# Attention scores on four array tiles at once, with groups of heads scheduled in twos: a block-summary attention followed by two feed-forward layers

## The chip, the cores and the metric

One core of one Trainium2 chip runs the whole kernel in one launch. The metric is device time in microseconds (us), from the runs of the compiled kernel; the profile shows one execution of it, whose span goes from the first to the last instruction. TensorE (PE) multiplies matrices into PSUM; VectorE (DVE), ScalarE (ACT) and GpSimd (POOL) do everything else; SyncE (SP) issues most of the DMAs. Each engine works through its own list of instructions in order.

## What is computed

An attention over a local window of 32 keys and over 24 block summaries, then two layers without bias. Shapes: q, k, v 2 x 8 x 768 x 64 (batch, head, token, dimension), w_in 512 x 2048, w_out 2048 x 512 for each layer; all fp32.

```python
k_sum = k.reshape(B, H, nb, 32, D).max(axis=3)
v_sum = v.reshape(B, H, nb, 32, D).mean(axis=3)
scores_l = where(abs(i - j) < 16, scale * q @ k.T, -1e9)
scores_s = scale * einsum('bhsd,bhnd->bhsn', q, k_sum) + log(32)
a = softmax(concat(scores_l, scores_s))
x = (a @ concat(v, v_sum)).transpose(0, 2, 1, 3).reshape(1536, 512)
h = x @ w_in;  x = maximum(0.01 * h, h) @ w_out          # layer 1
h = x @ moe2_w_in;  out = (h * tanh(softplus(h))) @ moe2_w_out   # layer 2
```

## The kernel before, in words

**Attention** is cut into 24 groups of 256 tokens of a pair of heads (`groups`: batch, chunk of 256 tokens, head pair). A group passes through these steps, each a function:

- `k_window` (POOL, L257): a tile `kw` of four windows, each 96 keys and the 24 block maxima of k from `k_sum` (DVE, L298).
- `scores` (PE, L362): 8 fp32 matmuls, for each of 4 blocks of 64 queries and each head of the pair. Head 0 lies in SBUF partitions 0 to 63, head 1 in 64 to 127, and their outputs go to the same partitions of PSUM, so the two heads use the two 64x64 tiles on the diagonal of the array. The result, 128 x 480, takes one PSUM bank.
- `score_max` (DVE, L374): adds the mask, scales, finds the row maximum, once for each of the 4 blocks; then the bank is free. `score_exp` (ACT, L384) with sums, `score_inv` (DVE, L393, L394), `score_norm` (POOL, L399).
- `p_transpose` (PE, L405) into another bank, `p_evac` (ACT L413 or DVE L415) to `pT`, `av` (PE, L424: 8 matmuls with a window of v and the v sums, into the same bank), `x_part` twice (a cast to fp32r, ACT L441 or DVE L443, and the remainder by subtraction, DVE L439). Then that bank is free.

The v sums come from `sum_v0` (PE, L317) for batch 0, spread to the four tiles `vw` by `place_v0` (DVE L327, ACT L329), and from `sum_vs` (DVE, L340) for batch 1.

**The layers** keep fp32 precision by high and low parts. A weight block is loaded as raw 64-bit words (`raw`), its top taken by ACT (`w_scale`, L130), merged on DVE (`w_merge`, L137), then split into a high part (`w_hi`, ACT L166 or DVE L164) and a low one (`w_lo`, POOL L173). `up` (PE, L458) makes one 128-wide block of h for 256 or 512 tokens in 12 matmuls, in two halves; `leaky_a` (ACT, L469, L470) and `leaky_b` (DVE, L474) make g; `down` (PE, L513) adds it into the four banks y0 to y3. One `up` is a slot; its `down` follows 3 slots later (`LAG`). Slots 0 to 5 have 256 tokens and need groups 0 to 3 (slots 0 to 2) and 4 to 7 (slots 3 to 5); slots 6 to 8 need groups 0 to 7, slots 9 to 14 groups 8 to 15, slots 15 to 20 groups 16 to 23.

**What sets the order.** Attention and slots 0 to 14 are not written in program order. `step(...)` notes every piece with an engine and a cost in us, what it needs, a `turn` (when it is due, counted in slots) and what it takes from `store` and gives back: PSUM banks, tiles `kw`, `s`, `pT`, raw buffers. `run_order` replays the steps in a time of its own, gives each free engine the ready step with the lowest turn, and so writes the list of each engine. The turn of a group's scores is `first_score[g]`, from the table `RATE`; its transposes and the product with v are due 0.3 slots later. Where TensorE would be idle before the first `up`, `warm` puts matmuls on a zero tile (L220). Banks: a0, a1 and y0 to y3 serve attention until slot 2 has been issued; from then on y0 to y3 belong to `down`, and a0 and a1 alone serve scores and transposes. From slot 15 on a plain loop writes the rest.

```python
            S1[g] = step({"PE": (1.15, 0)}, f, [KX[g], Q[g]], u, [("bank", ("S", g))], [("kw", g)])
            MX[g] = step({"dve": (0.88, 0)}, later(score_max, g), [S1[g]], u, [("s", ("s", g))], [("S", g)])
```

Of the kernel before, what the change touches and what calls it, by code (L numbers as in the profile page):

```python
# [28 lines left out]
def kernel(  # L29
# [34 lines left out]
    RATE = (2, 1, 1, 1, 1, 1, 2, 2, 1, 2, 1, 2, 1, 1)  # L64
# [142 lines left out]
    mask = ap1.tile([P, 6, WN], F32, name="mask")  # L207
# [53 lines left out]
    def k_window(g, part):  # L261
# [5 lines left out]
        w = ap2.tile([P, NB, WN], F32, tag="kw", bufs=3, name="kw")  # L267
# [98 lines left out]

    def score_max(g):
        b, c, hp = groups[g]
        pS = st[g]
        m0 = 0 if c == 0 else (2 if c == S // GT - 1 else 1)  # L370
# [2 lines left out]
        for n in range(NB):
# [44 lines left out]
    def av(g):  # L418
# [3 lines left out]
        for n in range(NB):  # L422
            for s in range(2):
# [144 lines left out]
    if True:  # L568
# [30 lines left out]
        first_score = {0: -4, 1: -4, 2: -4, 3: -4, 4: -1}  # L599
        g = 5  # L600
        for i, c in enumerate(RATE):
            for _ in range(c):
                first_score[g] = i
                g += 1
        assert g == NG
        X = len(RATE) + 1

# [7 lines left out]
        def step(on, fn, needs=(), turn=0.0, take=(), give=(), tag=None):  # L615
# [66 lines left out]
        for g in range(NG):  # L682
            b, c, hp = groups[g]
            u = first_score[g] + (g / 10 if g < 4 else 0)
            if g > 3:
                Q[g] = load(later(load_q, g, SP), 0.131, [S1[g - 4]], u - 2.5)
            KW[g] = step({"pool": (0.71, 1)}, later(k_window, g, 0), [K[b, hp]], u - 0.9, [("kw", ("kw", g))])
            KX[g] = step({"pool": (0.28, 1)}, later(k_window, g, 1), [KW[g], KS[b, hp]], u - 0.9)
            if g > 3:
                KW[g].needs.append((NM[g - 4], 0.07))  # L690

            def f(eng, g=g):
                scores(g, held["S", g])
            S1[g] = step({"PE": (1.15, 0)}, f, [KX[g], Q[g]], u, [("bank", ("S", g))], [("kw", g)])
            MX[g] = step({"dve": (0.88, 0)}, later(score_max, g), [S1[g]], u, [("s", ("s", g))], [("S", g)])
            EX[g] = step({"act": (1.6, 0)}, later(score_exp, g), [(MX[g], -0.5)], u)
            IV[g] = step({"dve": (0.39, 0)}, later(score_inv, g), [EX[g], MX[g]], u)
            NM[g] = step({"pool": (1.0, 1)}, later(score_norm, g), [IV[g]], u)

            def f(eng, g=g):  # L700
                p_transpose(g, held["T", g])
            TR[g] = step({"PE": (0.45, 0)}, f, [NM[g]], u + 0.3, [("bank", ("T", g))], [("s", g)])

            def f(eng, g=g):
                p_evac(g, eng)
            PT[g] = step({"act": (0.59, 0), "dve": (0.69, 0)}, f, [TR[g]], u + 0.3, [("pT", ("pT", g))])
            if g > 3:
                n = [AV[g - 4]]
                VW[g] = load(later(load_vw, g, SP), 0.196, n, u - 1.5)
                if (b, c) == (1, 0):  # L710
                    PLACE[b, hp] = step({"act": (0.83, 0)}, later(place_vs, hp), n + [VSS[4 * (hp // 2) + 3]], u - 0.5)
            AV[g] = step({"PE": (0.5, 0)}, later(av, g), [PT[g], VW[g], PLACE[b, hp]], u + 0.3, (), [("pT", g)])
            w = list(KX.values())[:12] if g >= 16 else []

            def f(eng, g=g):
                x_part(g, 0, eng)
            XH[g] = step({"act": (0.38, 0), "dve": (0.42, 0)}, f, [AV[g]] + w, u + 0.3)
            XL[g] = step({"dve": (0.43, 0)}, later(x_part, g, 1, None), [XH[g]], u + 0.3, (), [("T", g)])
# [294 lines left out]
```

## Time and profile before

| | |
|---|---|
| runs | 614.77, 614.79, 615.48 us; median 614.79 |
| span of the profiled execution | 612.8 us, 9138 instructions |
| its own time beside the span | not listed apart; the median of the runs is 2.0 us above the span |
| busy | PE 605.0, weight loads 492.2, DVE 386.0, ACT 314.6, POOL 196.1 us |
| DMA | 52.10 MB, mean 85 GB/s |
| granted TensorE clock | 1.00 |

A row of the timeline gives the start, the duration, engine, line, operation, result and inputs, partitions and elements, and how many such instructions were merged; in brackets stands what the engine waited for before it. TensorE lists fp32 matmuls as two instructions each, so 8 matmuls of a group are x16. Matmuls overlap: the time to the start of the next row is what a row costs, its own duration is longer by the end of the last matmul.

### The profile page before, as it was taken

The numbers are of one execution on the slowest core, as the hardware profiler recorded it, in microseconds if no ns is written. First come the engines' busy times: TensorE is split into PE (matmuls) and PEld (weight loads), VectorE is DVE, ScalarE is ACT, GpSimd is POOL, SyncE is SP. The second block draws the span as 40 slices with busy tenths as digits, with TensorE's granted clock in tenths as the row PEclk, the third lists the DMA queues.
The fourth block names the chain that finished last, engine by engine and source line by source line (L and its number), as shares of the span: only waits on it lengthen the run. The fifth ranks groups of instructions, "written<-read, shape, count | busy, mean of one in ns | idle before, by whom it ended". The sixth has DMA issues, their size and how long they took to land.

```text
span 612.8 us, 9138 instructions
## 1 busy us (share of the span) xinstructions
PE 605.0 (99%) x3330; PEld 492.2 (80%) x3330; DVE 386.0 (63%) x779; ACT 314.6 (51%) x669; POOL 196.1 (32%) x214
## 2 busy tenths in 40 slices
PE   9899999999999999999999999999999999999997
PEld 7788888778788888888888888888888888888886
DVE  6799775466242114112726798877689998678685
ACT  4786876457554123213656655454457555434442
POOL 6575673074330001001532133233231322332221
PEclk9999999999999999999999999999999999999999
DMA  9996463027541000001346410000012000001011
GB/s 320 344 287 224 135 207 113 2 94 247 164 156 60 1 1 1 0 1 34 110 137 235 130 43 1 0 1 0 1 40 99 0 1 1 1 18 52 1 70 68
DMA packets 19373, 52.10 MB, mean 85 GB/s; under 512 B 2176, under 2 KB 5248, under 8 KB 19072
## 3 DMA queue, kind: packets, MB, share of 16 engines
q1 hardware_dynamic: 18752, 51.00, 25.5%
q8 instruction: 26, 0.43, 0.3%
q10 hardware_dynamic: 576, 0.52, 0.3%
q14 instruction: 19, 0.16, 0.1%
HBM read 48.37 MB, written 3.15 MB: 84 GB/s over the span
## 4 chain that ended last, share of the span: by engine, by line
PE 89%; DMA 5%; DVE 3%; ACT 2%; issue 0%; POOL 0%; SPq 0%; DVEq 0%; ACTq 0%
PE h L458 41%; PE y L520 21%; PE y L513 20%; PE a L362 3%; DMA raw<-in_moe_w_in_dram 2%; PE a L424 2%; DMA v<-in_v_dram 2%; PE a L405 2%; DVE mid L137 1%; PE y L534 1%; ACT top L130 1%; DMA kT<-in_kT_dram 1%; DVE pT L415 0%; DVE ks L298 0%; DVE x L439 0%
## 5 line engine op out<-in xcount | busy, mean ns | idle before, releaser
L458 PE MATMUL h<-x,w 128*128 128x512 f32 (+1 forms) x1188 | 288.0, 388 | 0.0
L458 PEld LDWEIGHTS h<-x,w 128*128 128x128 f32 x1188 | 217.8, 188 | 48.9
L513 PE MATMUL y<-g,w 128*128 128x512 f32 (+1 forms) x612 | 145.9, 384 | 0.8 <-ACT yp L550 0.8
L520 PE MATMUL y<-w,g 128*128 128x512 f32 x552 | 136.9, 394 | 0.0
L194 POOL TENSOR_TENSOR g<-e,g 128x512 fp32r<-128x512 f32 x47 | 73.6, 1566 | 187.1 <-ACT g L191 175.8
L513 PEld LDWEIGHTS y<-g,w 128*128 128x128 f32 x612 | 109.8, 188 | 25.7 <-ACT yp L550 1.3
L520 PEld LDWEIGHTS y<-w,g 128*128 128x128 f32 x552 | 103.7, 188 | 24.1
L173 POOL TENSOR_TENSOR w<-mid,w 128x512 fp32r<-128x512 f32 x45 | 63.3, 1413 | 117.6 <-ACT w L166 113.8
L474 DVE TENSOR_TENSOR g<-t,g 128x512 fp32r<-128x512 f32 (+1 forms) x51 | 36.8, 721 | 90.9 <-ACT g L470 90.9
L137 DVE SCALAR_TENSOR_TENSOR mid<-raw,top 128x512 int32<-128x512 int32 x64 | 55.3, 869 | 33.1 <-POOL w L173 24.5
L469 ACT ACTIVATE t<-h 128x512 f32<-128x512 f32 (+1 forms) x51 | 28.9, 567 | 88.7 <-PE h L458 88.2
L130 ACT ACTIVATE top<-raw 128x512 f16<-128x512 bf16 x64 | 50.9, 795 | 38.1 <-DMA raw<-in_moe_w_out_dram 15.3
L485 ACT ACTIVATE e<-h 128x512 f32<-128x512 f32 x48 | 28.7, 598 | 68.9 <-PE h L458 62.3
L496 DVE SCALAR_TENSOR_TENSOR u<-u,r 128x512 f32<-128x512 f32 x48 | 36.9, 769 | 25.5 <-ACT r L489 25.2
L488 ACT ACTIVATE r<-u,two 128x512 f32<-128x512 f32 x48 | 34.8, 724 | 30.5 <-DVE u L487 30.5
L384 ACT ACTIVATE s<-s,nm 128x120 f32<-128x120 f32 x96 | 36.7, 385 | 16.0 <-DVE nm L374 12.1
L166 ACT CAST w<-mid 128x512 fp32r<-128x512 f32 x61 | 37.0, 614 | 8.6 <-DVE mid L137 4.2
L191 ACT CAST g<-e 128x512 fp32r<-128x512 f32 x48 | 29.5, 615 | 19.4 <-DVE e L498 19.1
L399 POOL TENSOR_TENSOR s<-s,r 128x480 f32<-128x480 f32 x24 | 25.1, 1047 | 33.1 <-DVE r L394 27.7
L487 DVE SCALAR_TENSOR_TENSOR u<-e 128x512 f32<-128x512 f32 x48 | 34.6, 720 | 1.1
L497 DVE SCALAR_TENSOR_TENSOR u<-u,r 128x512 f32<-128x512 f32 x48 | 33.1, 691 | 1.4
L498 DVE SCALAR_TENSOR_TENSOR e<-e,u 128x512 f32<-128x512 f32 x48 | 33.1, 689 | 1.1
(70 smaller groups left out, 467.2 us busy)
## 6 DMA issues: line engine op xcount, KB each, us to landing
raw<-in_moe_w_in_dram SPq DMA_DIRECT2D x32, 512.0 KB, 3.9
raw<-in_moe_w_out_dram SPq DMA_DIRECT2D x32, 512.0 KB, 3.8
vw<-in_vW_dram SPq DMA_DIRECT2D x24, 192.0 KB, 5.2
kT<-in_kT_dram SPq DMA_DIRECT2D x8, 400.0 KB, 7.0
out_dram<-yp SPq DMA_DIRECT2D x12, 256.0 KB, 2.0
q<-in_qT_dram SPq DMA_DIRECT2D x20, 128.0 KB, 4.0
vS<-in_vS_dram SPq DMA_DIRECT2D x2, 1024.0 KB, 7.1
v<-in_v_dram SPq DMA_DIRECT2D x2, 768.0 KB, 9.4
```

The lines of the kernel that those rows point to most:

```text
L130: nc.scalar.mul(out=do, in_=di, mul=4.0)
L137: nc.vector.scalar_tensor_tensor(out=d, in0=wraw.pop(i)[:, 0:2 * DM].rearrange("p (f w) -> p f w", w=2)[:, :, 1], scalar=13, in1=wtop.pop( ...
L166: nc.scalar.copy(out=w[:, 0], in_=wmid[i])
L173: (eng or nc.gpsimd).tensor_sub(out=w[:, 1], in0=wmid.pop(i), in1=w[:, 0].bitcast(F32))
L194: (nc.vector if lo == "dve" else nc.gpsimd).tensor_sub(out=dst_lo, in0=src, in1=dst_hi.bitcast(F32))
L384: nc.scalar.activation(out=s[:, n], in_=s[:, n], func=AF.Exp, scale=-1.0, bias=nm[:, n:n + 1], accum_out=sm[:, n:n + 1],)
L458: nc.tensor.matmul(ph[:, 0:n], w[:, a, kt * P:(kt + 1) * P], x[:, c, kt, o:o + n], start=(kt == 0 and i == 0), stop=(kt == KT - 1 and i == 2),
L474: nc.vector.tensor_sub(out=g[:, 1, 0:n], in0=t[:, 0:n], in1=g[:, 0, 0:n].bitcast(F32))
L488: nc.scalar.activation(out=r, in_=u, func=AF.Ln, bias=two[:, 0:1])
L496: V.scalar_tensor_tensor(out=u, in0=u, scalar=2.0, in1=r, op0=ALU.add, op1=ALU.mult)
L513: mm = nc.tensor.matmul(y[d][:, o:o + n], w[:, a, d * P:(d + 1) * P], g[:, c, 0:n], start=sta and not second, stop=sto,)
L520: nc.tensor.matmul(y[d], g[:, a, d * P:(d + 1) * P], w[:, c], start=sta, stop=sto,)
```

## The change

`scores` takes one group or two. For each pair of blocks and each head it issues two matmuls with the same SBUF partitions, whose outputs go to the lower and the upper half of the PSUM partitions: all four 64x64 tiles of the array are used. Tiles of different heads write to different banks, so there is a bank for each head (`pS[0]`, `pS[1]`), and a group fills half of both. The first four groups are scored one by one, the other twenty in ten pairs. In a pair, `score_max`, `score_exp` and the transposes stay steps of one group, while `scores` and `av` are one step for both; both banks are given back when the second mask pass is done. Order of rows within `s` changes from block to head and block, so the mask has 3 variants in place of 6 and `av` picks other columns. The table `RATE` now lists the turns of the ten pairs; `kw` has 4 buffers for 3, the dummy tile is 128 columns wide, and `run_order` can hand out two banks to one step. In the changed file lines after `scores` stand 7 lower: L362 is L367, L405 L412, L424 L431, L458 L465, L513 L520.

```diff
-    RATE = (2, 1, 1, 1, 1, 1, 2, 2, 1, 2, 1, 2, 1, 1)
+    RATE = (-1.0, -0.5, 3.5, 4.0, 6.5, 7.0, 7.0, 9.5, 10.5, 13.0)
...
-    mask = ap1.tile([P, 6, WN], F32, name="mask")
+    mask = ap1.tile([P, 3, WN], F32, name="mask")
...
-    def warm(n, w=256):
+    def warm(n, w=128):
...
-        w = ap2.tile([P, NB, WN], F32, tag="kw", bufs=3, name="kw")
+        w = ap2.tile([P, NB, WN], F32, tag="kw", bufs=4, name="kw")
...
-    def scores(g, tag):
-
-        t = qin.pop(g)
-        w = kwin.pop(g)
-        pS = bank(tag)
-        for n in range(NB):
-            for s in range(2):
-                r = slice(s * D, (s + 1) * D)
-                nc.tensor.matmul(
-                    pS[r, n * WN:(n + 1) * WN], t[r, :, n], w[r, n, :], start=True, stop=True,
-                )
-        st[g] = pS
+    def scores(gs, tags):
+
+
+        pS = [bank(t) for t in tags]
+        for k, g in enumerate(gs):
+            t = qin.pop(g)
+            w = kwin.pop(g)
+            for m in range(NB // 2):
+                o = (k * (NB // 2) + m) * WN
+                for s in range(2):
+                    r = slice(s * D, (s + 1) * D)
+                    for e in range(2):
+                        n = 2 * m + e
+                        nc.tensor.matmul(
+                            pS[s][e * QB:(e + 1) * QB, o:o + WN], t[r, :, n], w[r, n, :], start=True, stop=True,
+                        )
+            st[g] = (pS, k)
...
+            h, m = divmod(i, NB // 2)
+            o = (k * (NB // 2) + m) * WN
+            v = 1 if c == 0 and m == 0 else (2 if c == S // GT - 1 and m == NB // 2 - 1 else 0)
             nc.vector.tensor_tensor_reduce(
-                out=s[:, n], in0=pS[:, n * WN:(n + 1) * WN], in1=mask[:, m0 + n],
-                scale=-1.0 / rscale, scalar=BIG, op0=ALU.add, op1=ALU.min, accum_out=nm[:, n:n + 1],
+                out=s[:, i], in0=pS[h][:, o:o + WN], in1=mask[:, v],
+                scale=-1.0 / rscale, scalar=BIG, op0=ALU.add, op1=ALU.min, accum_out=nm[:, i:i + 1],
             )
...
+        batches = [[g] for g in range(4)] + [[g, g + 1] for g in range(4, NG, 2)]
+        first_score = {g: u for gs, u in zip(batches, (-4, -4, -4, -4) + RATE) for g in gs}
+        X = 15
...
+            t = [("bank", ("S", gs[0], h)) for h in range(2)] + [("s", ("s", g)) for g in gs]
+            x = step(
+                {"PE": (1.3 if pair else 0.8, 0)}, f, [d[g] for g in gs for d in (KX, Q)], u, t, [("kw", g) for g in gs],
+            )
...
+                MX[g] = step(
+                    {"dve": (0.88, 0)}, later(score_max, g), [x] + ([MX[gs[0]]] if g > gs[0] else []), u, (),
+                    [("S", gs[0], h) for h in range(2)] if last else (),
+                )
...
+            y = step({"PE": (1.1 if pair else 0.6, 0)}, f, n, u + 0.3, (), [("pT", g) for g in gs])
```

Since `run_order` writes the lists, the change moves instructions on every engine. Three places follow, each before and then as changed; a name ends in the number of its allocation.

VectorE before the first layer matmul, around the first merge of weights (L137). Before:

```order
L327 COPY vw_99<-y_283 24x512
L443 CAST x_373<-y_263 128x256
L393 TENSOR_SCALAR r<-sm 128x4
L394 RECIPROCAL r<-r 128x4
L439 TENSOR_TENSOR x_373<-y_263,x_373 128x256
L443 CAST x_373<-a_343 128x256
L137 SCALAR_TENSOR_TENSOR mid<-raw,top_86 128x512
L439 TENSOR_TENSOR x_373<-a_343,x_373 128x256
```

As changed:

```order
L400 TENSOR_SCALAR r<-sm 128x4
L401 RECIPROCAL r<-r 128x4
L137 SCALAR_TENSOR_TENSOR mid<-raw,top_86 128x512
L400 TENSOR_SCALAR r<-sm 128x4
L401 RECIPROCAL r<-r 128x4
L327 COPY vw_99<-y_309 24x512
L422 COPY pT<-y_366 120x512
L450 CAST x_401<-a_269 128x256
```

The merge stood behind the copies to vw and two casts to x; now it stands ahead of them, between two reciprocals.

TensorE around the first layer-1 matmul (`h<-x`), with the scores of groups 4 and 5 (kw with q_102 and q_103). Before:

```order
L405 MATMUL a_422<-ident,s 120x128 x4
L362 MATMUL a_429<-kw,q_102 64x120 x8
L424 MATMUL a_422<-pT,vw_101 64x64 x8
L458 MATMUL h<-x_373,w 128x256 x6
L362 MATMUL a_474<-kw,q_103 64x120 x8
L362 MATMUL a_489<-kw,q_104 64x120 x8
```

As changed:

```order
L431 MATMUL y_366<-pT,vw_100 64x64 x8
L412 MATMUL a_420<-ident,s 120x128 x4
L465 MATMUL h<-x_401,w 128x256 x6
L431 MATMUL a_420<-pT,vw_101 64x64 x8
L367 MATMUL a_461<-kw,q_102 64x120 x2
L367 MATMUL a_462<-kw,q_102 64x120 x2
L367 MATMUL a_461<-kw,q_102 64x120 x2
L367 MATMUL a_462<-kw,q_102 64x120 x2
L367 MATMUL a_461<-kw,q_103 64x120 x2
```

The layer matmuls now stand ahead of the last single group's product with v, and the scores of groups 4 and 5, which stood on both sides of them, follow as one block that alternates between two banks.

TensorE from slot 6 to slot 7 (ups of 512 tokens). Before:

```order
L458 MATMUL h<-x_373,w 128x256 x12
L362 MATMUL a_972<-kw,q_102 64x120 x8
L458 MATMUL h<-x_373,w 128x512 x6
L405 MATMUL a_1009<-ident,s 120x128 x4
L513 MATMUL y_725<-g,w 128x256 x3
L513 MATMUL y_726<-g,w 128x256 x3
L424 MATMUL a_1009<-pT,vw_100 64x64 x8
```

As changed:

```order
L431 MATMUL a_947<-pT,vw_98 64x64 x8
L431 MATMUL a_955<-pT,vw_99 64x64 x8
L465 MATMUL h<-x_401,w 128x512 x12
L412 MATMUL a_1036<-ident,s 120x128 x4
L412 MATMUL a_1042<-ident,s 120x128 x4
L520 MATMUL y_728<-g,w 128x256 x3
L520 MATMUL y_729<-g,w 128x256 x3
L431 MATMUL a_1036<-pT,vw_100 64x64 x8
L431 MATMUL a_1042<-pT,vw_101 64x64 x8
```

Single groups stood between halves of ups and downs; now two transposes and two products with v stand together, and no scores are among these rows.

## Rows read from the trace of the kernel before

**Rows 1.** The page, busy time and share of the span of each engine, with instructions.

```profile
PE 605.0 (99%) x3330; PEld 492.2 (80%) x3330; DVE 386.0 (63%) x779; ACT 314.6 (51%) x669; POOL 196.1 (32%) x214
```

**Rows 2.** Stages: length, busy PE, PEld, DVE, ACT, POOL, then clock, DMA share, GB/s.

```profile
24.73:39.88 15.15, 14.67 (x191) 13.13 (x187) 12.54 (x54) 12.96 (x48) 11.34 (x18) 1.00 1.04 305
39.88:64.31 24.43, 24.36 (x248) 21.78 (x247) 23.94 (x78) 18.36 (x62) 13.72 (x24) 1.00 0.68 212
64.31:76.53 12.22, 12.22 (x151) 10.23 (x149) 8.91 (x43) 10.67 (x36) 8.80 (x14) 1.00 0.52 158
76.53:126.59 50.06, 50.06 (x429) 39.89 (x425) 25.90 (x111) 29.05 (x94) 18.25 (x28) 1.00 0.31 99
126.59:612.80 486.21, 481.75 (x2080) 389.62 (x2076) 298.25 (x436) 230.65 (x388) 129.59 (x86) 1.00 0.17 56
```

**Rows 3.** Timeline of TensorE: start us, us, engine, line, operation, tiles, count.

```profile
13.53 0.85 PE L317 MATMUL y<-v,ind 128*24 128x128 f32 x24
...
25.73 2.18 PE L362 MATMUL a<-kw,q 64*64 64x120 f32 x32
27.84 0.97 PE L458 MATMUL h<-x,w 128*128 128x256 f32 x6
...
38.73 1.22 PE L362 MATMUL a<-kw,q 64*64 64x120 f32 x16
39.88 0.97 PE L513 MATMUL y<-g,w 128*128 128x256 f32 x6
...
47.51 0.69 PE L424 MATMUL a<-pT,vw 120*64 120x64 f32 x16
48.13 0.99 PE L458 MATMUL h<-x,w 128*128 128x256 f32 x6
...
56.96 0.60 PE L405 MATMUL a<-ident,s 128*120 128x128 f32 x4
57.32 0.96 PE L513 MATMUL y<-g,w 128*128 128x256 f32 x6
```

**Rows 4.** The same timeline, cut at 13.70, 39.05 and 39.10 us.

```profile
13.53 0.42 PE L317 MATMUL y<-v,ind 128*24 128x128 f32 x8
...
38.73 0.50 PE L362 MATMUL a<-kw,q 64*64 64x120 f32 x4
...
38.73 0.62 PE L362 MATMUL a<-kw,q 64*64 64x120 f32 x6
```

**Rows 5.** Timeline of all engines up to the first layer-1 matmul.

```profile
15.86 0.85 PE L317 MATMUL y<-v,ind 128*24 128x128 f32 x24 [0.33 <-DMA v<-in_v_dram]
16.79 1.40 DVE L327 COPY vw<-y 24x512 f32<-24x512 f32 x2 [0.31 <-PE y L317]
...
18.28 1.17 ACT L329 COPY vw<-y 24x512 f32<-24x512 f32 x2 [0.75 <-PE y L424]
...
21.25 0.68 DVE L137 SCALAR_TENSOR_TENSOR mid<-raw,top 128x512 int32<-128x512 int32 x1
...
24.73 0.98 PE L458 MATMUL h<-x,w 128*128 128x256 f32 x6
```

**Rows 6.** Groups by shape, 0 to 131 us: count, busy us, mean ns, idle before.

```profile
L384 ACT ACTIVATE s<-s,nm 128x120 f32<-128x120 f32 x96 | 36.7, 385 | 16.0 <-DVE nm L374 12.1 <-POOL kw L257 3.6
L399 POOL TENSOR_TENSOR s<-s,r 128x480 f32<-128x480 f32 x24 | 25.1, 1047 | 33.1 <-DVE r L394 27.7 <-ACT pT L413 2.3 <-ACT vw L346 1.7
...
L439 DVE TENSOR_TENSOR x<-a,x 128x256 fp32r<-128x256 f32 x23 | 9.6, 423 | 4.7 <-ACT x L441 4.1
L340 DVE TENSOR_REDUCE vs<-vS 128x16 f32<-128x512 f32 x8 | 8.4, 1054 | 0.0
...
L415 DVE COPY pT<-a 120x512 f32<-120x512 f32 x11 | 7.6, 689 | 4.1 <-PE a L405 4.0
```

**Rows 7.** Timeline of VectorE: a mask pass of one group and what follows.

```profile
44.57 0.28 DVE L374 CUSTOM_DVE_ANT_0 s<-a,mask 128x120 f32<-128x120 f32 x1
...
45.38 1.81 DVE L298 TENSOR_REDUCE ks<-kT 128x24 f32<-128x768 f32 x2
```

More of the change, by code (lines that the diff above doesn't have):

```diff
@@ L205 @@
     kp = att.enter_context(tc.tile_pool(name="kp", bufs=4))
-    mask = ap1.tile([P, 6, WN], F32, name="mask")
+    mask = ap1.tile([P, 3, WN], F32, name="mask")
     vw = [ap1.tile([WN, NB, 2, D], F32, name=f"vw{i}") for i in range(H // 2)]
     idle = {}
-    def warm(n, w=256):
+    def warm(n, w=128):
         if not idle:
-            idle["t"] = ap1.tile([P, 256], F32, name="idle")
+            idle["t"] = ap1.tile([P, 128], F32, name="idle")
             nc.vector.memset(idle["t"], 0.0)
@@ L235, in build_const @@
         nc.gpsimd.memset(mask[:, 0, WK:WN], math.log(SB) * rscale)
-        nc.vector.tensor_copy(out=mask[:, 1:], in_=mask[:, 0:1].to_broadcast([P, 5, WN]))
-        nc.gpsimd.memset(mask[:, 0, 0:HALO], NEG * rscale)
-        nc.gpsimd.memset(mask[:, 5, WK - HALO:WK], NEG * rscale)
+        nc.vector.tensor_copy(out=mask[:, 1:], in_=mask[:, 0:1].to_broadcast([P, 2, WN]))
+        nc.gpsimd.memset(mask[0:QB, 1, 0:HALO], NEG * rscale)
+        nc.gpsimd.memset(mask[QB:P, 2, WK - HALO:WK], NEG * rscale)
         nc.gpsimd.memset(two, 2.0)
@@ L352 @@
     st = {}
[L354 to L365 removed]
+    def scores(gs, tags):
[13 more added lines that the diff above has]
+            st[g] = (pS, k)
     def score_max(g):
         b, c, hp = groups[g]
[L369 to L370 removed]
+        pS, k = st[g]
         s = ap2.tile([P, NB, WN], F32, tag="s", bufs=4, name="s")
         nm = ap2.tile([P, NB], F32, tag="nm", bufs=4, name="nm")
[L373 removed]
+        for i in range(NB):
+            h, m = divmod(i, NB // 2)
+            o = (k * (NB // 2) + m) * WN
+            v = 1 if c == 0 and m == 0 else (2 if c == S // GT - 1 and m == NB // 2 - 1 else 0)
             nc.vector.tensor_tensor_reduce(
[L375 to L376 removed]
+                out=s[:, i], in0=pS[h][:, o:o + WN], in1=mask[:, v],
+                scale=-1.0 / rscale, scalar=BIG, op0=ALU.add, op1=ALU.min, accum_out=nm[:, i:i + 1],
             )
@@ L426, in av @@
                     w[:, n, s, :],
-                    t[:, n, s * QB:(s + 1) * QB],
+                    t[:, s * (NB // 2) + n // 2, (n % 2) * QB:(n % 2 + 1) * QB],
                     start=True, stop=True,
@@ L575 @@
             load_k(0, hp, SP)
-        warm(5)
+        warm(10)
         build_const()
@@ L598 @@
         NI = len(items)
[L599 to L606, printed above, removed]
+        batches = [[g] for g in range(4)] + [[g, g + 1] for g in range(4, NG, 2)]
+        first_score = {g: u for gs, u in zip(batches, (-4, -4, -4, -4) + RATE) for g in gs}
+        X = 15
         steps = []
@@ L681 @@
         S1, KX, MX, EX, IV, NM, TR, PT, AV, XH, XL = ({} for _ in range(11))
[L682 to L718, printed above, removed]
@@ L720 @@
         for g in range(1, NG):
             for d in (KW, S1):
-                d[g].needs.append((d[g - 1], -9.0))
+                if d[g] is not d[g - 1]:
+                    d[g].needs.append((d[g - 1], -9.0))
         for i in range(2 * nA + 4):
@@ L847, in run_order @@
                     for name, key in x.take:
-                        have = store[name]
+                        have = list(store[name])
                         if name == "bank":
                             have = [y for y in have if y[0] == "a" or not closed[0]]
+                        for other, item in pick.values():
+                            if other == name:
+                                have.remove(item)
                         if not have:
```

44 lines of the change are left out of this document (43 added, 1 removed).

## The prediction

> **What bounds the kernel now.** First the table of busy times on the page: TensorE 605.0 of 612.8 us, the next engine, VectorE, 386.0 [rows 1]. Then the stages, over five stretches [rows 2]. TensorE is hardly idle after 24.73 us: 14.67 busy of 15.15, 24.36 of 24.43, then all of 12.22 and 50.06. So from the first layer-1 matmul (24.73 us, L458) on, time that TensorE no longer needs comes off the end, unless a wait takes its place. Before 24.73 us TensorE is filled with dummy matmuls (L220), and a chain through the other engines decides. The same table shows what lies closest behind: VectorE, busy 23.94 of 24.43 us between 39.88 and 64.31. The profiled span is 612.8 us, the median of the runs 614.79; the 2.0 us around the span I leave as they are, and take the sum off the median. The granted clock reads 1.00 in every stretch, so I charge no change of it.
>
> **The scores themselves.** One group takes 1.15 us from its first matmul to the next instruction's (38.73 to 39.88) and 16 passes: each of its 8 fp32 matmuls runs as two [rows 3]. Two passes (one on each diagonal 64x64 tile) are in flight at a time: the same row cut at two ends shows 4 passes in 0.50 us and 6 in 0.62 [rows 4], so a round is 0.12 us, and 8 rounds plus 0.19 us for changing over make the 1.15. The change puts four passes in a round. No row has four 64x64 tiles. Lower bound: the sums of v (L317) keep four column tiles in flight, 8 passes in 0.42 us and 24 in 0.85, which is 0.43 / 4 = 0.107 us a round [rows 3, 4], for passes of 128 columns instead of 120. Upper bound: no overlap, two groups in a row as now, 25.73 to 27.84, 2.11 us. I take the four-tile row, as the nearest, but the longer round of L362: a pair is 32 passes, 8 rounds of 0.12 plus 0.2, **1.2 us**; a single group 0.7.
>
> A rule speaks against it. The trace has column tiles that share all their rows with loads and matmuls overlapping: L424 does 16 passes between 47.51 and 48.13, 39 ns a pass, and L317 27 ns [rows 3, 4]. The Trainium skill (TensorE: Matmul & The Clock Gate, Part 3, what overlaps and what doesn't) says that a weight load overlaps running matmuls only where the row group differs; in the new order two neighbours always share their row group. By that rule a pair would stay near 2.1 us; by L317 and L424, where no row group differs, it does not hold here.
>
> **The sum, stage A, up to the first L458 matmul.** Now: the merge of the first weights (L137) is issued on VectorE only at 21.25, behind the casts to x; its cast and its low part follow, and TensorE begins at 24.73 [rows 5]. In the new order of VectorE that merge stands before the copies to vw (the first pair of fences above), so the weights are ready some 5 us sooner. What is late next is v: its second load releases L317 at 15.86, hidden by nothing, as before. From there: sums 0.85, first copy to vw on ScalarE 0.58, second on VectorE 0.70, two more on ScalarE 1.17 [rows 5], cast to x (taken as long as the subtraction) and subtraction 0.42 each [rows 6], a handover of some 0.05 before each: 15.86 + 4.14 + 0.2 = 20.2. Stage A: **-4.5 us**. Bounds: 0 (some queue still holds it) to -4.7 (no handover).
>
> **Stage B, from there to the first matmul of slot 8 (now 76.53).** The order lists between these two marks give the counts. The layer matmuls are the same (ups 0 to 7, downs 0 to 5). Scores: now 12 groups, then 6 pairs: 12 x 1.15 - 6 x 1.2 = 6.6 us less. Transposes: 11 then 8, at 0.36 (56.96 to 57.32) [rows 3] to 0.45 with a change of mode: 1.3 less. Products with v (L424): 11 groups at 0.62 = 6.8, then one group and 4 pairs; a pair is 16 rounds less one changeover, 1.1: 5.0, so 1.8 less. Sum 9.7 less TensorE work; it now takes 51.8 us with 0.55 idle (15.15 - 14.67 and 24.43 - 24.36), so 41.5 are left.
>
> New waits must be added, because pairs come in lumps. I follow the first two pairs with durations of rows: exponentials 4 x 0.385 a group on ScalarE, the scaling 1.05 on GpSimd, the copy of the transposed tile 0.69, a sum of v 1.05 [rows 6], the mask pass of a group 0.8 (44.57 to 45.38) [rows 7]. (1) The first pair takes both banks a0 and a1, and a1 still holds the last single group until its x is written: v product, 0.6, cast and subtraction 0.85, so TensorE waits 1.0. (2) The low weights of slot 1: 0.3. (3) The transpose of group 5: its exponentials end some 3.6 us after the pair's mask begins, its reciprocal is queued on VectorE behind the mask pass of group 6, then the scaling; TensorE has 0.4 of transposes left: 1.0. (4) The paired v product waits for both copies, and that of group 4 sits on VectorE behind the mask pass of group 7 and a sum of v: 1.3. (5) Low weights of down 0: 0.4, and 0.5 of small change. Together 4.5 us. From slot 3 on the ups and downs between two steps of a pair (1.5 us and more each) are longer than what the pair waits for. Stage B: 41.5 + 4.5 - 51.8 = **-5.8 us**. Bounds: no waits (-10.3) and twice the waits (-1.3).
>
> **Stage C, slot 8 to the end of attention (now 126.59).** Work moved here from B comes back: 3 transposes (+1.3), 6 pairs of v products for 9 groups (+1.0); 4 pairs of scores for 7 groups, 4.8 for 8.05 (-3.3). **-1.0 us**, no waits: VectorE has 25.90 of 50.06 us busy [rows 2]. After it the same instructions run; TensorE works 481.75 of 486.21 us there, and what it waits for starts from the end of attention, so it moves along.
>
> Edits at nothing: the smaller mask (its copy shrinks to two fifths, on VectorE before k has landed); the fourth kw buffer; dummy matmuls of 128 columns, twice as many; q loads, which SP issues by groups as before and whose release comes sooner.
>
> Sum: -4.5 - 5.8 - 1.0 = -11.3. **614.8 - 11.3 = 603.5 us.** With the upper price of a pair instead (2.11) 10 x 0.9 = 9 us of it are lost; with twice the waits 4.5.
>
> **Rivals.**
> 1. VectorE becomes the bound in the middle. For: 23.94 of 24.43 us busy now, just where TensorE would be hurried. Against: by my walk its list from the leaky halves of slots 0 and 1 to that of slot 5 is 22 us of work from about 36 (5 sums of v, 4 block maxima, 4 mask passes, 5 merges, 9 writes of x and smaller ones) and ends near 59, and the down that needs it begins near 62; the margin is 3 to 4 us. If copies and reductions queue worse than that, some 4 to 5 us of stage B go: about 608. The Trainium skill (TensorEngine Tiling (Array Packing), PSUM Bottleneck) says the same in general: tiling speeds up TensorE, not the reading of PSUM. By it this rival would be the likeliest; the idle half of VectorE in stage C speaks against its lasting. Chance 0.14.
> 2. The change does not do what it says: the two tiles of one row group run one after the other, since nothing in the trace has four 64x64 tiles. A pair then costs 2.1, and of the 11.3 us 9 are lost: 612.5, give or take 2, since longer scores also cover some of the waits counted in B. (By the rule on weight loads above, this would come first; L424 and L317 speak against it.) Chance 0.07.
> 3. **Slower:** the two banks. After the downs begin only a0 and a1 serve attention; now scores and transposed tile take one each, a pair takes both for each of its two turns. If each pair made TensorE wait at its scores or its transposes, the 11.3 us are gone at 1.1 us a pair (10 pairs); at 2.0 us a pair the time is 603.5 + 20 = 623.5. For: the two turns hold the banks some 3 and 5 us of an average 8 to 10 us a pair. Against: the new order puts at least one up or down (1.5 to 3 us) before nearly every turn after slot 3, and the wait is no longer than the rest of a mask pass or a subtraction. Chance 0.06.
> 4. It goes better: fewer waits in B than I count, 600 to 602. Chance 0.10.
>
> **How the numbers follow.** Forecast 0.63, with 602 to 606 as its own spread; the rivals as above. 0.2% (1.2 us) is what a measurement can tell here, so faster is below 613.6: 0.63 + 0.14 + 0.10 and 0.03 of rival 2, **0.90**; same is the rest of rival 2, 0.04; slower rival 3, 0.06. The range takes the forecast, rival 1 and what of rival 4 lies above 600.8: 600.8 to 609.0, some 0.8.
>
> **What would show it.** Four passes start together, and 32 passes fill about 1.2 us to the next instruction; the first layer-1 matmul near 20.2; slot 8 near 66 instead of 76.53; TensorE's waits between 20 and 40 us at the first transposes and the v product, 4 to 5 us in all, none to speak of after; the end of the last v product some 11 us before 126.59. It would be wrong if a round takes 0.2 us or more, if VectorE's sums of v or copies stand last in waits after 40 us, or if waits at a0 and a1 recur with every pair.

## The result, and the profile after

| | before | changed |
|---|---|---|
| runs, us | 614.39 to 615.48, median 614.78 (4) | 606.32 to 608.53, median 606.69 (4) |
| profiled execution: time, span | 614.8 by the median, 612.8 | 608.53, 606.4 |
| forecast | | 603.5 (600.8 to 609.0) |

The ratio is 0.9877, 95% interval 0.9861 to 0.9893: 8.1 us faster at the medians, 3.2 us slower than the forecast. The profiled execution is the slowest of the four, 1.8 us above the median; its span is 6.4 us shorter than that of before, where the sum had 11.3. The next rows look for the missing 4.9.

The page of the changed kernel, TensorE's busy time and share (it answers to [rows 1]):

```profile
PE 596.3 (98%) x3334; PEld 485.9 (80%) x3334; DVE 382.4 (63%) x777; ACT 314.1 (52%) x671; POOL 194.0 (32%) x214
```

Its stages up to the wait at 181 us, cut at its own marks (first layer-1 matmul 21.42, slot 8 at 69.61, end of the last product with v 129.03); columns as in [rows 2], the third from the right is the granted clock:

```profile
21.42:32.30 10.88, 8.49 (x115) 6.88 (x113) 8.37 (x46) 9.51 (x39) 7.24 (x12) 1.00 1.03 332
32.30:39.20 6.90, 6.39 (x53) 6.28 (x54) 6.09 (x12) 3.02 (x8) 3.90 (x12) 0.51 0.85 270
39.20:69.61 30.41, 30.10 (x374) 26.80 (x373) 26.22 (x95) 25.89 (x85) 18.12 (x24) 1.00 0.64 216
69.61:129.03 59.42, 59.42 (x546) 47.43 (x544) 33.81 (x137) 34.51 (x117) 21.90 (x38) 1.00 0.30 95
129.03:181.13 52.10, 50.36 (x219) 40.02 (x215) 29.80 (x36) 35.21 (x62) 27.29 (x19) 1.00 0.60 202
```

Three places differ from what was forecast. TensorE is idle for 2.4 us of the first stretch; in the second the granted clock is 0.51, that is the 1.2 GHz level, where before it read 1.00 everywhere; and between 129 and 181 us TensorE waits again.

TensorE's timeline of the changed kernel, in brackets what it waited for (it answers to [rows 3] and [rows 5]):

```profile
13.01 1.11 PE L412 MATMUL a<-ident,s 128*120 128x128 f32 x4
14.05 0.48 PE L367 MATMUL a<-kw,q 64*64 64x120 f32 x2
...
15.98 0.65 PE L412 MATMUL y<-ident,s 128*120 128x128 f32 x4
16.56 0.87 PE L220 MATMUL h<-idle 64*64 64x128 f32 x6
17.36 0.86 PE L317 MATMUL y<-v,ind 128*24 128x128 f32 x24
...
21.42 0.96 PE L465 MATMUL h<-x,w 128*128 128x256 f32 x6
...
24.17 1.22 PE L367 MATMUL a<-kw,q 64*64 64x120 f32 x28 [0.72 <-DVE x L446]
...
26.71 0.73 PE L465 MATMUL h<-x,w 128*128 128x256 f32 x4 [0.16 <-POOL w L173]
...
30.39 1.32 PE L412 MATMUL a<-ident,s 128*120 128x128 f32 x8 [0.87 <-DVE nm L381]
32.81 1.98 PE L431 MATMUL a<-pT,vw 120*64 120x64 f32 x32 [1.10 <-DVE pT L422]
34.72 2.93 PE L465 MATMUL h<-x,w 128*128 128x256 f32 x12
37.44 1.91 PE L412 MATMUL a<-ident,s 128*120 128x128 f32 x8
...
41.91 1.46 PE L520 MATMUL y<-g,w 128*128 128x256 f32 x10 [0.31 <-POOL w L173]
...
44.01 1.23 PE L367 MATMUL a<-kw,q 64*64 64x120 f32 x32
45.17 1.70 PE L520 MATMUL y<-g,w 128*128 128x256 f32 x12
...
127.95 1.15 PE L431 MATMUL a<-pT,vw 120*64 120x64 f32 x32
...
175.29 4.10 PE L465 MATMUL h<-x,w 128*128 128x512 f32 x17
181.13 3.02 PE L520 MATMUL y<-g,w 128*128 128x512 f32 x12 [1.74 <-ACT yp L557]
```

A pair of scores takes 1.16 us (44.01 to 45.17), forecast 1.2. By the rule of the Trainium skill that was weighed (TensorE: Matmul & The Clock Gate, Part 3, what overlaps and what doesn't) it would have stayed at 2.1; the row decides against it.

The rows of before at the same places, from its timelines of TensorE and then of ScalarE, with the one wait that TensorE has between slot 8 and the last of these rows (155.92):

```profile
12.94 0.65 PE L405 MATMUL y<-ident,s 128*120 128x128 f32 x4
...
125.97 0.69 PE L424 MATMUL a<-pT,vw 120*64 120x64 f32 x16
...
155.92 1.67 PE L513 MATMUL y<-g,w 128*128 128x512 f32 x6 [0.84 <-ACT yp L550]
...
183.70 4.09 PE L458 MATMUL h<-x,w 128*128 128x512 f32 x17
187.63 2.91 PE L513 MATMUL y<-g,w 128*128 128x512 f32 x12
...
127.11 2.18 ACT L166 CAST w<-mid 128x512 fp32r<-128x512 f32 x4
```

And ScalarE's timeline of the changed kernel at the same places:

```profile
129.51 2.18 ACT L166 CAST w<-mid 128x512 fp32r<-128x512 f32 x4
...
178.25 0.80 ACT L130 ACTIVATE top<-raw 128x512 f16<-128x512 bf16 x1 [3.99 <-DMA raw<-in_moe_w_out_dram]
...
180.48 1.08 ACT L557 ACTIVATE yp<-y 128x512 f32<-128x512 f32 x2
```

The 17 matmuls (x17) are the same in both programs and have the same work before them. There the changed kernel leads by 183.70 - 175.29 = 8.4 us; at the next row by 187.63 - 181.13 = 6.5. So 1.9 us of the gain are given back between 175 and 181 us: L520 waits for the copies of y (L557), which stand on ScalarE behind a cast (L130) that waits 3.99 us for a load of weights. The last product with v comes at 127.95 us, **later** than before (125.97), though TensorE is some 8 us ahead; the first weights of the second pass are split right behind it, at 129.51 instead of 127.11.

### The profile page after: what moved, and what is told of

The parts are those of the page before. It is cut to its first block, busy times and chain, and to the rows that moved or that the text cites. A ratio compares the mean times of both kernels' runs of the same rounds, so it can differ in the third digit from the quotient of the medians.

```text
span 606.4 us, 9153 instructions
## 1 busy us (share of the span) xinstructions
PE 596.3 (98%) x3334; PEld 485.9 (80%) x3334; DVE 382.4 (63%) x777; ACT 314.1 (52%) x671; POOL 194.0 (32%) x214
## 4 chain that ended last, share of the span: by engine, by line
PE 89%; DMA 4%; ACT 3%; DVE 2%; POOL 1%; issue 1%; SPq 0%; DVEq 0%; ACTq 0%
PE h L465 40%; PE y L527 21%; PE y L520 19%; DMA raw<-in_moe_w_out_dram 3%; PE a L431 2%; PE a L367 2%; PE a L412 2%; ACT top L130 1%; DVE mid L137 1%; PE y L541 1%; PE h L220 1%; DMA kT<-in_kT_dram 1%; POOL w L173 1%; DMA raw<-in_moe_w_in_dram 1%; ACT g L477 0%
## 5 line engine op out<-in xcount | busy, mean ns | idle before, releaser
L465 PE MATMUL h<-x,w 128*128 128x512 f32 (+1 forms) x1188 | 289.7, 390 | 0.2 <-POOL w L173 0.2
L465 PEld LDWEIGHTS h<-x,w 128*128 128x128 f32 x1188 | 219.0, 189 | 49.7 <-ACT g L477 0.4
L520 PE MATMUL y<-g,w 128*128 128x512 f32 (+1 forms) x612 | 145.6, 384 | 2.1 <-ACT yp L557 1.7
L520 PEld LDWEIGHTS y<-g,w 128*128 128x128 f32 x612 | 110.0, 188 | 26.8 <-ACT yp L557 2.2
L481 DVE TENSOR_TENSOR g<-t,g 128x512 fp32r<-128x512 f32 (+1 forms) x51 | 34.5, 679 | 89.6 <-ACT g L477 89.6
L137 DVE SCALAR_TENSOR_TENSOR mid<-raw,top 128x512 int32<-128x512 int32 x64 | 55.3, 871 | 29.9 <-POOL w L173 23.7
L130 ACT ACTIVATE top<-raw 128x512 f16<-128x512 bf16 x64 | 50.6, 796 | 29.0 <-DMA raw<-in_moe_w_out_dram 12.6
```

Of the source, the lines that this page charges most:

```text
L130: nc.scalar.mul(out=do, in_=di, mul=4.0)
L137: nc.vector.scalar_tensor_tensor(out=d, in0=wraw.pop(i)[:, 0:2 * DM].rearrange("p (f w) -> p f w", w=2)[:, :, 1], scalar=13, in1=wtop.pop( ...
L465: nc.tensor.matmul(ph[:, 0:n], w[:, a, kt * P:(kt + 1) * P], x[:, c, kt, o:o + n], start=(kt == 0 and i == 0), stop=(kt == KT - 1 and i == 2),
L520: mm = nc.tensor.matmul(y[d][:, o:o + n], w[:, a, d * P:(d + 1) * P], g[:, c, 0:n], start=sta and not second, stop=sto,)
```

## The experiments

c1 is the changed kernel again; e1 to e11 each change it further. There are two theories at first. **A**: the missing gain is TensorE's clock. **B**: other chains (copies, weights, loads) set these times whatever the clock. Two more, on what waits at 180 us, come later. The table gives marks of the profiled executions (us from the start of the span): first layer-1 matmul; second part of the first down (in the changed kernel the row at 41.91); the x17 row; "next", the row behind it, 3.93 later where nothing waits; "split", the first split of second-pass weights.

| run | median us | layer 1 | down | x17 | next | split |
|---|---|---|---|---|---|---|
| before | 614.78 | 24.73 | | 183.70 | 187.63 | 127.11 |
| changed | 606.69 | 21.42 | 41.91 | 175.29 | 181.13 | 129.51 |
| c1 | 607.61 | 21.30 | 41.80 | 174.79 | 179.94 | 129.21 |
| e1 | 607.24 | 23.30 | 40.98 | 174.38 | 179.26 | 128.52 |
| e2 | 608.14 | 21.10 | 41.06 | 174.68 | 179.47 | 128.65 |
| e3 | 609.68 | 23.23 | 43.19 | 177.34 | 181.89 | 131.63 |
| e4 | 606.84 | 21.19 | 38.91 | 172.21 | 178.35 | 126.30 |
| e5 | 608.44 | 21.87 | 41.01 | 174.53 | 181.50 | 128.49 |
| e6 | 611.80 | 20.71 | 38.39 | 178.97 | 185.01 | 132.89 |
| e8 | 604.75 | 22.48 | 40.14 | 173.54 | 177.47 | 117.56 |
| e9 | 603.75 | 21.34 | 39.07 | 172.43 | 176.36 | 116.49 |
| e10 | 603.20 | 20.63 | 38.35 | 172.20 | 176.13 | 115.81 |
| e11 | 610.71 | 19.56 | 38.07 | 179.65 | 183.58 | 122.48 |

(e7 has another order and is told below.) c1 to e3, e4 to e7, e8 to e10 and e11 each shared a chip and runs of the kernel before (medians 614.41, 614.69, 614.12 and 614.32 us); ratios are to these.

**c1: the changed kernel again.**

> The changed kernel as it is, again, beside which the next three are read. Expected: 606.3 to 607.5 us; both theories say the same. In its profile TensorE's first transposes again run at half rate (1.04 us for four of group 0, against 0.59 before), and the granted clock is 0.50 over some us between 30 and 40 us in most executions.

606.47 to 610.36, median 607.61 us, ratio 0.9884 (0.9860 to 0.9909). Its profile has the same half clock, and a wait of 1.06 us where the first profile had 1.74.

**e1: more dummies early.**

```diff
             def f(eng, gs=gs):
+                if gs[0] < 2:
+                    warm(2)
                 scores(gs, [held["S", gs[0], h] for h in range(2)])
```

> Two dummy matmuls more ahead of each of the first two groups' scores, so that TensorE has no gap there and runs at 2.4 GHz from some 10.3 us on, as before the change, and not from 15.3. Theory A (the TensorE clock is what the forecast lacked): the second sum of v, whose data landed at 14.0 us, starts by 16.4 instead of 17.36, and the first layer-1 matmul at 20.2 to 20.5 instead of 21.42; the time falls by 0.8 to 1.3 us. Theory B (the copies of v, the weights and the DMAs set these times whatever TensorE's clock): below 0.4 us.

TensorE had no gap any more and still came to full rate later, at some 18.5 us (the expectation of e5 puts it at 17.5), as its timeline shows:

```profile
17.38 1.11 PE L412 MATMUL y<-ident,s 128*120 128x128 f32 x4
...
32.28 1.32 PE L412 MATMUL a<-ident,s 128*120 128x128 f32 x8 [0.89 <-DVE nm L381]
34.71 1.15 PE L431 MATMUL a<-pT,vw 120*64 120x64 f32 x32 [1.11 <-DVE pT L422]
35.79 1.71 PE L465 MATMUL h<-x,w 128*128 128x256 f32 x12
...
40.98 1.46 PE L520 MATMUL y<-g,w 128*128 128x256 f32 x10 [0.38 <-POOL w L173]
```

The dummies only pushed the first layer-1 matmul 2.0 us back. Yet the time is not worse (607.24, ratio 0.9880, 0.9854 to 0.9906). That is in the bounds of B, but not for B's reason: in this execution the clock did not fall behind the same two waits: the 12 matmuls of a slot took 1.55 us (35.79 to the next row at 37.34), not 2.72, and from the transposes to the down's second part it is 40.98 - 32.28 = 8.70 us, in c1 41.80 - 30.28 = 11.52. So the half clock costs **2.8 us**; it was found by accident, and e4 tests it.

**e2, e3: dummies in the two waits, alone and with e1.**

```diff
...
+                            if x is TR[4] or x is AV[4]:
+                                z = [v for v in store["bank"] if v[0] == "y"][-1]
+                                y = Step()
+                                y.fn, y.eng, y.begin, y.end = later(fill, 8 if x is TR[4] else 12, z), "PE", t, t
+                                out.append(y)
```

(`fill`, not shown, issues that many matmuls of 128 columns on the zero tile.)

> Dummy matmuls (8 and 12, of 0.11 us each) into a free bank ahead of the transposes of group 4 and of the product with v of groups 4 and 5, where TensorE waits 0.87 and 1.10 us. Theory A: the granted clock stays at 1.00 through 30 to 40 us, the work there (a slot, 8 transposes) takes 1.5 and 0.8 us instead of 2.7 and 1.6, and the time falls by 1.5 to 3 us. Theory B: the clock stays up, but the low weights of the first down, which TensorE waits for at 41.9 us, come no sooner; the wait there grows by what was saved and the time falls by 0.5 us or less.

> Both edits together. Theory A: the sum of the two, 2.5 to 4 us below the changed kernel, 602.5 to 604.3 us, close to the 603.5 of the forecast. Theory B: less than 0.8 us below it.

The dummies were mis-sized: each is two passes of 0.118 us, so 8 took 1.88 us, not 0.87, and 12 took 2.77. In e2 the clock stayed at 1.00 and the slot took 1.54 us, but TensorE reached it at 35.88, some 2.1 us later than with dummies of the right size (33.73 in e4); the two nearly cancel (down 0.7 us earlier than in c1). The times are 608.14 us for e2 (ratio 0.9862 to 0.9913) and 609.68 for e3 (0.9890 to 0.9946, with both overruns and the early dummies). Neither decides between A and B.

**e4: the same, half as many** (4 and 5 in place of 8 and 12).

> The late fill again, sized by what the first try showed (16 passes of the dummies took 1.88 us, not 0.87): 4 dummies ahead of the transposes of group 4 and 5 ahead of the product with v of groups 4 and 5, 0.95 and 1.2 us. Theory A (the half clock from 32 to 39 us is a loss on the path): the second part of the first down starts some 2.5 us earlier than the 41.80 of the repeat, at 39.0 to 39.6, slot 8 at some 67 instead of 69.5, and the time falls by 1 to 2.8 us, as far as the weights of the second pass, which TensorE waited for at 180 us (1.06 us there), let it through. Theory B: the first down waits for its low weights as long as before; 0.4 us or less.

TensorE's timeline, then a window of it with the clock:

```profile
29.22 1.08 PE L92 MATMUL y<-idle 64*64 64x128 f32 x8
...
31.41 1.30 PE L92 MATMUL y<-idle 64*64 64x128 f32 x10
...
38.91 1.46 PE L520 MATMUL y<-g,w 128*128 128x256 f32 x10 [0.38 <-POOL w L173]
...
172.21 4.10 PE L465 MATMUL h<-x,w 128*128 128x512 f32 x17
178.35 4.61 PE L520 MATMUL y<-g,w 128*128 128x512 f32 x12 [2.05 <-ACT yp L557]
```

```profile
178.00:183.00 5.00, 4.65 (x13) 3.69 (x14) 2.41 (x4) 3.06 (x6) 1.28 (x1) 0.66 0.11 15
```

A holds up to 172 us: the down is 2.9 us earlier, and the lead at the x17 row is 11.5 us, the 11.3 of the forecast. Then 3.9 us are lost: 2.2 up to the next row, by a wait of 2.05 at the copies of y, and 1.7 in its 12 matmuls, which take 4.61 us for 2.91, with the clock at 0.66. The median is 606.84 (ratio 0.9856 to 0.9887), which can't be told from c1's. In its profile, what the middle gains is taken back at 180 us.

**e5: the first dummies of 256 columns again.**

```diff
...
-        warm(10)
+        warm(5)
```

(The default is `w=256` again, and the zeros lie in `tops[1]`, a tile that is there anyway.)

> One part undone: the first dummy matmuls are 5 of 256 columns again in place of 10 of 128 (their zeros lie in a tile that is there anyway). The late rise of the clock was not due to gaps, since with the gaps filled it came at 17.5 us instead of 15.4. If the width of the dummies is what delays it, TensorE runs at full rate from 10.3 to 11 us as before the change, the second sum of v starts by 16.0 us and the first layer-1 matmul by 20.1 (21.30 in the repeat). If the shorter scores are what delays it, it still comes near 15 us and nothing moves by more than 0.2. On the time: 0 to 1 us less, unless the earlier start lets the clock fall later as it does in the changed kernel.

The width is not it: the first layer-1 matmul comes at 21.87, full rate at some 16.4 us. The time is 608.44 us (605.12 to 608.91), with a wait of 2.87 us at the copies of y.

**e6: two tiles in the new order.**

```diff
...
-                            pS[s][e * QB:(e + 1) * QB, o:o + WN], t[r, :, n], w[r, n, :], start=True, stop=True,
+                            pS[k][r, n * WN:(n + 1) * WN], t[r, :, n], w[r, n, :], start=True, stop=True,
```

(The loops have blocks outside and heads inside, and mask and `av` go back to the columns of before; not shown.)

> Same order of work, same pairs, but the scores use only the two diagonal tiles, as before the change (a bank for each group, the old columns in the product with v). Theory: a pair then takes 2.1 us instead of 1.16, ten pairs lose 9.5 us of TensorE; some of it fills the waits between 24 and 33 us (0.72 and 0.87) and that at 180: 613 to 616 us, so that nearly all of the gain is the four tiles. Rival: the gain is the new order (weights merged sooner, pairs, less switching) and the tiles bring half of it or less: below 611 us.

611.80 us, ratio 0.9957 (0.9940 to 0.9973): between the two, only 4.2 us over c1, and still 2.9 faster than before, so that much of the gain needs no four tiles. But three things moved with the tiles. The clock reads 1.00 throughout, which gives 2.8 back; full rate came at some 10.2 us and layer 1 0.6 earlier; longer scores filled 1.5 us of waits between 22 and 42 us. 9.5 - 2.8 - 0.6 - 1.5 = 4.6, against 178.97 - 174.79 = 4.2 at the x17 row. That is a reckoning, which e11 tests.

**e7: four tiles, no pairs.**

```diff
-        batches = [[g] for g in range(4)] + [[g, g + 1] for g in range(4, NG, 2)]
+        batches = [[g] for g in range(NG)]
```

(The turns are those of the old table.)

> Four tiles, but no pairs: every group alone, by the old table of turns, with half of two banks. A group then costs 0.7 instead of 1.15, which is 20 x 0.45 = 9 us less than before and 20 x 0.1 = 2 us more than with pairs; but every group takes a0 and a1 both, so TensorE waits for the mask pass of the one before (0.8 us and its queue) wherever two groups stand close. Theory (pairs are what makes two banks enough): waits at the banks of 0.3 to 0.8 us for many groups, 610 to 618 us. Rival (the shorter lumps even save the waits of 0.87 and 1.10 us at the first pairs): 605 to 608 us.

Worse than either expectation: 625.90 us, ratio 1.0188 (1.0169 to 1.0206). Its timeline, one of the waits ahead of scores and the end:

```profile
43.94 1.03 PE L367 MATMUL a<-kw,q 64*64 64x120 f32 x16 [0.79 <-DVE nm L381]
...
187.40 4.10 PE L465 MATMUL h<-x,w 128*128 128x512 f32 x17
196.60 5.39 PE L520 MATMUL y<-g,w 128*128 128x512 f32 x12 [5.10 <-ACT yp L557]
```

3.7 us are lost up to the x17 row (187.40 against 183.70), by waits ahead of scores and a half clock near 35 us; the larger loss is again at the copies of y, a wait of 5.10 us and slow matmuls behind it (5.39 us for 2.91).

All the runs so far lose 0.6 to 5.3 us at that one place. The table says why, if the last column is taken off the x17 row: before, 183.70 - 127.11 = 56.6 us lie between the first split of second-pass weights and that row; in every profiled execution of c1 to e6 it is 45.6 to 46.1, and 37.9 in e7, which has the longest wait. The same weights have 10 us less. (What makes the wait 0.44 us in e3 and 2.87 in e5 with the same 46 us is not shown.) Theory **C**: the split waits for the end of attention, and that is now late in TensorE's order. Its rival **D**: the loads of weights have a pace of their own, wherever attention ends. For C the kernel has two possible reasons, which the runs don't separate: these weights' tiles come from a pool (`post`) that is opened when attention's pools are closed, and in ScalarE's list the split stands behind attention's last cast.

**e8: the last pair's turn.** The lists of the order have what was overlooked: the last product with v stood behind 168 layer-1 and 132 layer-2 matmuls before, and behind 186 and 157 in the changed kernel.

```diff
-    RATE = (-1.0, -0.5, 3.5, 4.0, 6.5, 7.0, 7.0, 9.5, 10.5, 13.0)
+    RATE = (-1.0, -0.5, 3.5, 4.0, 6.5, 7.0, 7.0, 9.5, 10.5, 12.0)
```

> One number: the turn of the last pair, 12.0 for 13.0. In TensorE's order its product with v then stands behind 168 layer-1 and 132 layer-2 matmuls, as before the change, and not behind 186 and 157. Theory C (the weights of the second pass get their room in SBUF only when attention ends; before the change the first of them were split from 127.1 us on, in the changed kernel from 129.5, while TensorE came there 8 us sooner, so that it meets them at 180 us): the splitting starts near 119 us, the wait at the copies of y near 180 us (1.74 and 1.06 us) is gone, and the lead of 8.4 to 8.9 us at 164 us lasts to the end: 605.4 to 606.2 us. Rival D (the loads of the weights set the pace, 512 KB in 3 to 5 us, wherever attention ends): the wait stays, 606.5 to 607.6 us.

604.75 us, ratio 0.9856 (0.9839 to 0.9872), better than expected. TensorE, and ScalarE's first split:

```profile
173.54 4.09 PE L465 MATMUL h<-x,w 128*128 128x512 f32 x17
177.47 2.91 PE L520 MATMUL y<-g,w 128*128 128x512 f32 x12
...
117.56 2.18 ACT L166 CAST w<-mid 128x512 fp32r<-128x512 f32 x4
```

The splitting starts 11.9 us sooner than in the changed kernel, 56.0 us ahead of the x17 row, the next load of these weights is issued at 121.67 instead of 133.57, and the wait is gone, by one number that moves no work in or out: C holds, D falls. But in this execution the clock did not fall either, so part of its lead of 10.2 us, and perhaps of the median, is not the turn's doing. e9 against e4, both with the clock held, is the clean pair.

**e9: e8 and e4 together.**

> The last pair at 12.0 and the late fill by halves together. The late fill alone led by 11.5 us at 164 us (8.9 in the repeat) and gave 3.9 of it back between 178 and 183 us. Theory C: nothing is given back, 602.8 to 603.8 us, at the forecast of 603.5. Rival D: 606 to 607 us, as with the late fill alone.

603.75 us, ratio 0.9834 (0.9819 to 0.9849), as C said; e4 had 0.9871 (0.9856 to 0.9887). The lead is 11.3 us at the x17 row (172.43) and 11.3 behind it:

```profile
176.36 2.91 PE L520 MATMUL y<-g,w 128*128 128x512 f32 x12
```

**e10: and whole-array dummies.**

```diff
-            nc.tensor.matmul(idle["p"][0:QB, 0:w], t[0:D, 0:QB], t[0:D, 0:w], start=True, stop=True)
+            nc.tensor.matmul(idle["p"][:, 0:w], t, t[:, 0:w], start=True, stop=True)
```

> As the run before, and the dummy matmuls ahead of the first layer-1 matmul use all 128 rows and columns of the array instead of one 64x64 tile, with the same 128 columns of data. With two-tile scores TensorE came to full rate at some 10.5 us, with four-tile scores, which are over sooner and leave more of the time to one-tile dummies, at 14.7 to 17.5. If it is the share of the array in use that brings the clock up, it comes by 8 to 11 us here, the second sum of v starts at 16.0 us or sooner (17.1) and the first layer-1 matmul by 20.0 (21.2): 1 us less than the run before, 601.8 to 603. If not, the same 602.8 to 603.8; a loss of 1 to 2 us if whole-array passes take longer than 0.21 us at the low clock.

603.20 us, ratio 0.9821 (0.9806 to 0.9836): the fastest version, beyond both kernels. Its time can't be told from that of e9, but its rows can:

```profile
5.40 0.75 PE L367 MATMUL a<-kw,q 64*64 64x120 f32 x16
...
15.35 0.85 PE L317 MATMUL y<-v,ind 128*24 128x128 f32 x24 [0.45 <-DMA v<-in_v_dram]
...
20.07 0.22 PE L431 MATMUL y<-pT,vw 120*64 120x64 f32 x1 [1.04 <-issue]
```

Full rate is there from the first scores at 5.40 us (0.75 us long, 1.09 in c1), and the second sum of v waits for its data again. It starts 1.9 us sooner than in e9 (17.28), layer 1 only 0.7 sooner (20.63); 1.04 of the difference is an idle time ahead of one matmul, "issue", for which the profile names nothing.

**e11: two tiles in that version.**

> The run before (whole-array dummies, late fill by halves, last pair at 12.0; 603.2 us) with the scores on the two diagonal tiles again, and nothing else changed. With two tiles in the changed kernel itself only 4.2 us were lost (611.8 against 607.6), not 9.5. Theory (the four tiles are worth the whole price, 10 pairs at 0.95, and the changed kernel lost the rest of it to the clock, to waits that longer scores fill, and to the weights at 180 us): here, where the clock stays up and nothing waits at 180 us, 8 to 9.5 us are lost less the 0.7 of the one wait left at the first pair: 610.5 to 612.7 us. Rival (a two-tile pair costs less than two groups did, and the new order alone carries half of the gain): below 609 us.

610.71 us, ratio 0.9932 (0.9919 to 0.9946). A pair of scores in it:

```profile
40.17 2.18 PE L367 MATMUL a<-kw,q 64*64 64x120 f32 x32
42.29 1.70 PE L520 MATMUL y<-g,w 128*128 128x256 f32 x12
```

2.12 us a pair against 1.16: ten cost 9.6. 1.1 of it comes back at layer 1 (19.56 against 20.63) and 0.9 by two waits that longer scores fill (0.71 and 0.16), which leaves 7.6; found are 179.65 - 172.20 = 7.45 at the x17 row and 7.5 between the medians. The parts agree less well than the sum: up to the last product with v the difference is 6.7 us (120.97 - 114.30), and 0.8 comes behind it, where TensorE waits for copies of y in both, 0.49 us in e10 (143.21) and 1.08 in e11 (151.88). So the four tiles are worth some 7 us in this version. The other 3.6 us of it (e11 against before) are the new order, the weights' earlier merge and the dummies, which no run takes apart further.

## Why the prediction was right, and where it fell short

- **Price of a pair, right.** A pair takes 1.16 us for 1.2 forecast, and 2.12 with two tiles in the same order (e11); the round of L362 was the right row to take. Rival 2 (the tiles of one row group run one after the other) falls.
- **Stage A, -4.5 forecast, -3.3 found.** The chain was as described, but it began at 17.36 instead of 15.86. The term "its second load releases L317 at 15.86" was the wrong one: the loads landed sooner than before, at most 8.4 us after an issue at 5.6 or sooner, so by 14.0 (by 15.8 before), as the view of that tile shows (line, issues, and time from issue to landing); TensorE came late to them, since it had not yet come to full rate: the first transposes took 1.04 us (13.01 to 14.05), before the change 0.59 (12.94 to 13.53, [rows 3]). With two-tile scores it came earlier again (e6: 10.2 us, layer 1 at 20.71), with dummies of 256 columns it did not (e5).

```profile
L87 SPq DMA_DIRECT2D v<-in_v_dram x2: 379/411/443, 4.7 to 5.6; - x2
...
DMA to landing us min/median/max: 7.1/7.8/8.4
```
- **Stage B, -5.8 forecast, -3.6 found** (slot 8 at 69.61). The waits named are there, each at its place: 0.72, 0.16, 0.87, 1.10 and 0.31, forecast 1.0, 0.3, 1.0, 1.3 and 0.4. Their sum is 3.2 instead of 4.0 (4.5 with the 0.5 of small change), so better. The step that failed is "the granted clock reads 1.00 in every stretch, so I charge no change of it": behind the waits the clock fell to half (with dummies in them it did not, e4), and the half clock cost 2.8 us (e1 against c1), 2.6 by the x17 row of e4. The rest is the work itself: 48.2 us less 3.2 of waits and 2.8 of clock leaves 42.2, where the sum had 41.5.
- **Stage C, -1.0 forecast, about -0.7 found.** From slot 8 to the x17 row before takes 107.17 us, the changed kernel 105.68: 1.49 less, of which 0.84 is the wait of before at 155.92, which the changed kernel does not have. With the clock kept up, the lead at the x17 row is 11.5 us (e4), the forecast 11.3. That it fits so well is partly luck: in e4 stage A brings 3.5 (4.5 forecast), B 6.4 (5.8), C 0.75 (1.0), and the wait of before, which was in no term, 0.84.
- **"What it waits for starts from the end of attention, so it moves along", wrong,** and so was "the end of the last v product some 11 us before 126.59": it came at 129.03, 2.4 us after. TensorE's gain came forward, the end of attention did not, and the weights of the second pass, which are split only behind it, met TensorE at 180 us. e8 shows it by one number, e9 with the clock held. The order lists had said it; the text ahead of the result quotes them only up to slot 7. With stages A (1.2 short), B (2.2 short) and C (0.5 better, the wait of before taken in) the 1.9 us given back at 180 us make 4.8 of the 4.9 us that were missing.
- **Rivals 1 and 3** didn't come: after 42 us no wait names a mask pass, a sum of v, or a bank of a pair. That the banks are near their limit is seen in e7, not in pairs.

The range held since it reached to 609. Its upper part was meant for VectorE (rival 1), and it covered two losses that the prediction did not have, the half clock and the late weights: that the time lies inside is luck as far as these go.

## What to carry to other kernels

A gain on the bounding engine is worth what the next resource lets through: look where the freed stage *ends* in the new order, and what starts only behind it, up to the last instruction and not only where the change is thick. Lumps of work make waits, and a wait on TensorE costs more than its own length if the clock falls behind it (2.8 us here behind waits of 0.87 and 1.10). With a few dummy matmuls in them, sized by a row of this same kernel, the clock stayed up there in six executions of six (e2, e3, e4, e9, e10, e11). Give an experiment its own profile: two of these (e1, e6) would have been misread by their times alone, and in e8 the profile shows that part of the gain may be the clock's.

## What was not expected of the hardware

- Early on the granted clock reads 1.00 in every window while four transposes take 1.04 us (13.01), and 0.58 at 15.98: that column did not show the slow start here; the durations do. A window of the changed kernel, with the columns of [rows 2]:

```profile
10.00:15.00 5.00, 5.00 (x47) 4.12 (x45) 2.99 (x13) 2.61 (x12) 3.71 (x8) 1.00 1.05 357
```

- TensorE came to full rate by the first scores at 5.4 us behind whole-array dummies (e10, e11), at some 10.2 us with two-tile scores and one-tile dummies (e6), and at 14.6 to 18.5 with four-tile scores, which are over sooner, and one-tile dummies (ten profiled executions), with gaps or without (e1), with dummies of 128 columns or 256 (e5). The Trainium skill (TensorE: Matmul & The Clock Gate, Part 1) says that warming up takes an amount of time and not a number of matmuls; no one amount of time, counted from the first dummies, fits these three.
- Behind the same waits of 0.87 and 1.10 us the clock fell in three executions without late dummies (the changed kernel, c1, e5) and not in two others (e1, e8), in which full rate had come last of the five, at some 18.5 and 17.7 us. At 180 us it fell behind a wait of 2.05 us (e4) and not behind one of 2.87 (e5: the 12 matmuls take 3.02). What decides this stays open.
